# Attention, a dense layer and a routed layer of eight experts: half of the first expert's products set between the last routing's, and range checks, one weight piece and routing placed elsewhere

## The chip, the cores and the metric

One core of one Trainium2 chip. The metric is device time in microseconds (us) of one execution, the median of several; lower is better. Engines are TensorE (PE, with its weight loads as PEld), VectorE (DVE), ScalarE (ACT), GpSimd (POOL) and SyncE (SP, which issues most DMAs).

## What is computed

Three layers, each on the output of the one before; 4 sequences of 768 positions, 3072 tokens of 384 values.

```python
# 1: a gated linear recurrence for each of 8 heads of 48
for t in range(S):
    S_re, S_im = ar * S_re - ai * S_im + kv, ar * S_im + ai * S_re
    y[:, :, t] = einsum('bhd,bhde->bhe', q[:, :, t], S_re)
# 2: a product of two projections to 1536, and one back
x = ((x @ w_a) * (x @ w_b)) @ w_out
# 3: tokens with x @ w_skip > 0 go to the one expert with the largest logit
e_idx = argmax(xc @ w_gate, axis=1)
y[mask] = gate_w[mask, None] * (maximum(xc[mask] @ w1[e], 0) @ w2[e])   # 384 -> 1024 -> 384
out[do_compute] = xc + y
```

## The kernel before

The recurrence is worked in 24 units of 128 positions (6 chunks of 4 sequences), two units to a group, 12 groups. A group's 256 tokens then go through the dense layer (`moe1`): twelve steps f, each with 18 products of 256 columns for `ab{g}_f` and six of 394 columns (`op`, L631 to L633) for the step before last. All products work on operands split into a high and a low part in `fp32r`, three products for one. Between them, DVE and ACT make `asb`, `gh`, `gl` of the step, and the trigonometry, exponentials and masks of the next group's units.

The last ten of the 394 columns are the gate and skip logits. Routing of a group has three parts: `pick` (the expert's one-hot `rt_oh`, and on PE the prefix sums `pp`), `weigh`, and `place` (`sl`, the comparison of a row's position with 256 slots, and on PE the products `pt` that add the group's tokens to the slot table `tbl`; for the last group `pt` for the indices `giu` and `pg` for the gate values). The `xr` rows of a group are written to a table `xd` in DRAM (L676) and to `out`.

Each expert takes 256 slots: `gather` fetches two times 128 rows of `xd` by indirect DMAs on POOL, `tokens` transposes them on PE (`xgp`) and splits them (`xgt`), `hidden` makes eight blocks of nine products of 256 columns (`eh`, L954 to L957), with a Relu on ACT (`hh`) and the low part on DVE (`hl`), and `second` six products of 384 columns for each block (`eo`, L971 to L973, into two banks, one for each 128 rows). The first expert's weights (`wq0` to `wq3`) are in place in group 11; the next ones are loaded into `stg` (six loads of 768 KB, gated by a small POOL copy from the first gathered rows) and converted by `convert`, ACT making the high part and DVE or POOL the low one.

The order on each engine is a scheduler's, held by rows of names: `ORDER` for the start, `STEADY` for the groups from 3 on, with a word such as `asb{g}_1` for one instruction; `chain` ties each named instruction behind the one before. `PLACE` (a row for each operation, `wl` being the low part of the ten logit columns `wo` takes from `w2s`, L532) names the engine of an instruction where it isn't the usual one.

Two things need checks that the reference doesn't have: `least` and `largest` (L285, L288) test the range of `a_re` and `a_im`. Units 0 to 5 are tested late, by `check_late` in groups 2 to 4: a second load into `chk` (one buffer, L294, behind `ts` of a later unit), then the test on DVE. If a test fails, or an expert has more than 256 tokens, a slow branch is taken behind the main block.

`warm` issues bf16 products of 128x256 that nobody reads: 10 behind group 11's last product, 6 behind its prefix sums, 24 behind the gate products, 13 and 8 behind the first expert's two transposes, 61 in all (`WARMS`, `WARMX`, L837).

Of the kernel before, what the change touches and what calls it, by code (L numbers as in the profile page):

```python
# [10 lines left out]
F32 = mybir.dt.float32  # L11
F32R = mybir.dt.float32r
# [48 lines left out]
    "wl": {"vector": (1, 4,)},  # L61
# [15 lines left out]
WARMS = (10, 6, 24)  # L77
WARMX = (13, 8)
ENGINES = {getattr(mybir.EngineType, x) for x in ("PE", "Activation", "DVE", "Pool")}
GF = 5  # L80
PORT = 8
ROWS = 64
# [14 lines left out]
    "DVE": "q{u} k{u} q{v} k{v} t4_{u} asb{g}_0 lg{p}*2 tl{u} t4_{v} gl{g}_0 tl{v} asb{g}_1 t3_{u}*2 gl{g}_1 t4_{u} asb{g}_2 qr{u}:1 kr{u}:1 gl{g}_2 t3_{v}*2 qr{u}:0 kr{u}:0 asb{g}_3 t4_{v} gl{g}_3 kr{v}:1 asb{g}_4 kr{v}:0 gl{g}_4 qr{v}:1 qr{v}:0 asb{g}_5 gl{g}_5 sc{u}_0 sc{u}_1 xt{n} asb{g}_6 gl{g}_6 t1_{x} t1_{y} asb{g}_7 t1_{x} ll{x} gl{g}_7 t1_{y} ll{y} asb{g}_8 gl{g}_8 sc{v}_0 sc{v}_1 im{x} imp{x} im{y} imp{y} xt{n} asb{g}_9 gl{g}_9 re{a} re{b} asb{g}_10 gl{g}_10 asb{g}_11 gl{g}_11",  # L97
}


def keep_rows(nc, after):
# [34 lines left out]
def kern(tc, q, k, v, a_re, a_im, w_a, w_b, w_out, w_skip, w_gate, w1, w2, out):  # L136
# [3 lines left out]
    with st:  # L140
# [148 lines left out]

        def check_late(i):  # L290
            c, b = units[i]
            for src, test in ((a_re, least), (a_im, largest)):
# [3 lines left out]
                test(i, t)  # L296
# [329 lines left out]
        def moe1_out(g, f, gh, gl):  # L626
# [7 lines left out]
            if f == NF - 1:  # L634
                moe1_end(g)
                if g == NG - 1:
                    warm("m", i.ins, WARMS[0])

        def moe1_step(g, f):
# [15 lines left out]
            dve.tensor_tensor(out=asb, in0=ab[:, 256:], in1=asb, op=ALU.mult)  # L655
# [10 lines left out]
        def moe1_end(g):  # L666
# [40 lines left out]
        def pick(g, behind=None, spare=None):  # L707
            if g == NG - 1:
                whole()
# [28 lines left out]
            if g == NG - 1:  # L738
                warm("p", i.ins, WARMS[1])
# [55 lines left out]
        def slots(tiles, tag, sls, last=False, spare=None):  # L795
# [29 lines left out]
            warm("t", ins.ins, WARMS[2])  # L825

# [163 lines left out]
        def experts(first):  # L990
# [21 lines left out]
            for e in range(2):  # L1012
                gather(e)
# [282 lines left out]
```

## Time and profile before

| | us |
|---|---|
| median of 3 runs | 832.45 (832.26 to 834.45) |
| the profiled execution | 831.85 |
| its span | 830.0 |
| PE busy | 786.5 |
| PEld busy | 754.2 |
| DVE busy | 550.4 |
| ACT busy | 453.0 |
| POOL busy | 167.6 |

The mean granted clock of PE is 0.997 of full speed. The times of single instructions come from the profiled execution, so sums are made against its 831.85 us. Matmuls are pipelined: the time of one in a row is longer than the distance between the starts of two. PE's idle time is the first thing to look for, then what released PE at its end.

### The profile page before, as it was taken

Reading aid. Unit: us, or ns where it says so; the run is one execution under the profiler, and the core shown is the slowest. Engines: PE = TensorE matmul, PEld = TensorE weight load, DVE = VectorE, ACT = ScalarE, POOL = GpSimd, SP = SyncE. Lnnn points to the kernel's source line nnn. Section 1 sums busy time; section 2 is a strip of 40 time slices with the busy share of each in tenths; the row PEclk is TensorE's granted clock in tenths of the full one; section 3 lists DMA queues with packets and bytes.
Section 4 is the critical chain, followed back from the end, with each engine's and each line's share of the span. In section 5 each row is a group of like instructions: output and inputs, shape, how many; then the busy total and the mean of one; then the engine's idle time right before and its main releaser. Section 6 shows DMA issues by size and latency. Waiting matters only on the chain.

```text
span 830.0 us, 22382 instructions
## 1 busy us (share of the span) xinstructions
PE 786.5 (95%) x9115; PEld 754.2 (91%) x9115; DVE 550.4 (66%) x1417; ACT 453.0 (55%) x949; POOL 167.6 (20%) x196
## 2 busy tenths in 40 slices
PE   1899999999999999999999999999999999999995
PEld 0589899999989989999999999998999989999995
DVE  7999888685676857757676576746747347555541
ACT  6897655473546644566455565555535226555540
POOL 3131443410100000000000000000003026666650
PEclk9999999999999999999999999999999999999998
DMA  9995223251342432213222231120105049667500
GB/s 253 251 316 121 54 63 68 46 122 33 77 89 38 106 64 72 54 36 87 51 68 55 52 81 36 50 49 11 40 18 176 1 164 338 215 222 208 180 22 23
DMA packets 180960, 83.17 MB, mean 100 GB/s; under 512 B 152084, under 2 KB 168026, under 8 KB 180848
## 3 DMA queue, kind: packets, MB, share of 16 engines
q1 hardware_dynamic: 178800, 76.26, 35.7%
q0 software_dynamic: 2048, 5.40, 1.8%
q8 instruction: 73, 1.20, 0.6%
q14 instruction: 39, 0.32, 0.1%
HBM read 69.84 MB, written 12.61 MB: 99 GB/s over the span
## 4 chain that ended last, share of the span: by engine, by line
PE 80%; DVE 6%; DMA 6%; ACT 3%; issue 2%; POOL 1%; SPq 0%; POOLq 0%; DVEq 0%; ACTq 0%
PE ab L647 11%; PE ab L648 10%; PE ab L649 10%; PE op L632 5%; PE op L631 5%; PE op L633 5%; PE y L502 4%; PE eh L954 3%; PE eh L955 3%; PE eh L957 3%; PE eo L971 3%; PE eo L972 3%; PE eo L973 3%; DMA chk<-in_a_im_dram 2%; PE pcs L461 2%
## 5 line engine op out<-in xcount | busy, mean ns | idle before, releaser
L647 PE MATMUL ab<-xt,wa 128*128 128x256 f32 x432 | 124.4, 288 | 0.5 <-DVE asb L655 0.4
L647 PE MATMUL ab<-xt,wb 128*128 128x256 f32 x432 | 123.0, 285 | 0.1
L648 PE MATMUL ab<-xt,wb 128*128 128x256 f32 x432 | 122.5, 284 | 0.0
L649 PE MATMUL ab<-xt,wb 128*128 128x256 f32 x432 | 122.4, 283 | 0.0
L649 PE MATMUL ab<-xt,wa 128*128 128x256 f32 x432 | 121.7, 282 | 0.0
L648 PE MATMUL ab<-xt,wa 128*128 128x256 f32 x432 | 121.6, 281 | 0.0
L659 DVE TENSOR_TENSOR gl<-asb,gh 128x256 fp32r<-128x256 f32 x131 | 62.6, 478 | 64.0 <-ACT gh L279 63.9
L632 PE MATMUL op<-wo,gh 128*128 128x394 f32 x288 | 99.2, 344 | 1.7 <-POOL wo L532 1.7
L633 PE MATMUL op<-wo,gh 128*128 128x394 f32 x288 | 98.7, 343 | 0.0
L631 PE MATMUL op<-wo,gl 128*128 128x394 f32 x288 | 98.5, 346 | 0.0
L279 ACT ACTIVATE asb<-ab 128x256 f32<-128x256 f32 x139 | 52.5, 378 | 68.8 <-PE ab L649 65.2
L647 PEld LDWEIGHTS ab<-xt,wa 128*128 128x128 f32 x432 | 81.4, 188 | 2.4 <-ACT asb L279 0.7
L648 PEld LDWEIGHTS ab<-xt,wb 128*128 128x128 f32 x432 | 81.5, 189 | 1.1 <-issue 1.0
L655 DVE TENSOR_TENSOR asb<-ab,asb 128x256 f32<-128x256 f32 x144 | 60.0, 417 | 33.3 <-ACT asb L279 33.1
L647 PEld LDWEIGHTS ab<-xt,wb 128*128 128x128 f32 x432 | 81.4, 188 | 0.6 <-DVE wb L532 0.3
L649 PEld LDWEIGHTS ab<-xt,wb 128*128 128x128 f32 x432 | 81.3, 188 | 0.7 <-issue 0.6
L648 PEld LDWEIGHTS ab<-xt,wa 128*128 128x128 f32 x432 | 81.4, 188 | 0.5 <-DVE xt L514 0.2
L649 PEld LDWEIGHTS ab<-xt,wa 128*128 128x128 f32 x432 | 81.5, 189 | 0.3 <-issue 0.2
L922 POOL TENSOR_TENSOR wq<-stg,wq 128x768 fp32r<-128x768 f32 x32 | 59.5, 1861 | 95.7 <-DMA stg<-in_moe_w_dram 46.4
L279 ACT ACTIVATE gh<-asb 128x256 fp32r<-128x256 f32 x132 | 54.4, 413 | 36.3 <-DVE asb L655 36.1
L264 POOL MEMSET v<- 128x64 f32 x24 | 3.5, 150 | 339.0 <-PE y L502 246.3
L961 DVE SCALAR_TENSOR_TENSOR hl<-eh,hh 128x256 fp32r<-128x256 f32 x64 | 27.1, 424 | 52.9 <-ACT hh L960 52.8
(268 smaller groups left out, 2021.2 us busy)
## 6 DMA issues: line engine op xcount, KB each, us to landing
stg<-in_moe_w_dram SPq DMA_DIRECT2D x28, 768.0 KB
rawa<-in_moe_w_a_dram SPq DMA_DIRECT2D x6, 768.0 KB
re<-in_a_re_dram SPq DMA_DIRECT2D x24, 192.0 KB
rawb<-in_moe_w_b_dram SPq DMA_DIRECT2D x6, 768.0 KB
q<-in_q_dram SPq DMA_DIRECT2D x24, 192.0 KB
k<-in_k_dram SPq DMA_DIRECT2D x24, 192.0 KB
rawo<-in_moe_w_out_dram SPq DMA_DIRECT2D x6, 768.0 KB
xd<-xr SPq DMA_DIRECT2D x24, 192.0 KB
```

The costliest lines, as they stand in the source:

```text
L279: return act.activation(out=out, in_=in_, func=AF.Copy) if e is act else e.tensor_copy(out, in_)
L502: ins = pe.matmul(o, l[:, col : col + STRIP], r, start=begin, stop=end).ins
L631: pe.matmul(o, gl[:, ts], wh, start=f == 0, stop=False)
L632: pe.matmul(o, gh[:, ts], wl, start=False, stop=False)
L633: i = pe.matmul(o, gh[:, ts], wh, start=False, stop=f == NF - 1)
L647: pe.matmul(o, wl, xt[:, c, 0], start=c == 0, stop=False)
L648: pe.matmul(o, wh, xt[:, c, 1], start=False, stop=False)
L649: pe.matmul(o, wh, xt[:, c, 0], start=False, stop=c == NCC - 1)
L655: dve.tensor_tensor(out=asb, in0=ab[:, 256:], in1=asb, op=ALU.mult)
L659: on("gl", n).tensor_tensor(out=gl, in0=asb, in1=gh, op=ALU.subtract)
L922: lo.tensor_tensor(out=o[:, 1], in0=t, in1=o[:, 0], op=ALU.subtract)
L961: vm = dve.scalar_tensor_tensor(out=gl, in0=o, scalar=0.0, in1=gh, op0=ALU.max, op1=ALU.subtract)
```

## The change

- `wl` names piece 3 for DVE; DVE's row of `ORDER` has `wo3` between the two `kr3`, and POOL's row loses it.
- `STEADY` holds from group 2 on. In its DVE row the second `t1_{y}` stands ahead of `ll_{x}`, and the table's addition `tbl:{r}` is named ahead of `asb{g}_9`. The trigonometry of units 6 and 7 is issued in two steps, as that of later pairs.
- The late tests are tied one by one behind `asb` of steps 1, 4, 7 and 10 of groups 2 to 4.
- New rows `LAST` (PE) and `LAST_DVE` set the end of group 11. Routing of group 10 fills a first half of expert 0's slots; its 128 rows are gathered in group 11 (`gather_half`, by `gi0`, a copy of the indices), and transposed behind `ab11_10`. A third flag, `good[:, 2]`, says that these 128 slots are all taken; if not, the slow branch is run. The rows of group 10 are also written over group 11's places of `xd`, two writes of 192 KB more, before group 11's own.
- Expert 0's products for f = 0 to 5 are made for each 128 rows apart: `front(h, x)`, 36 products of 128 columns for x = 0 and 18 for x = 1 (`fa{h}_x`), with a Relu and a low part of 128x512 and 128x256; `back(h, f)`, three of 384 columns. `front(0, 0)`, `front(0, 1)` and three `back(0, f)` stand between the last routing's products; the others, `hidden(0, 6)`, `hidden(0, 7)` and their `second` follow when the second half is gathered. From expert 1 on the loop is as before. Only one gather, of the second half, stands ahead of expert 1's two, and the loads of `stg` are gated on it.
- The 61 warming products are gone.

```diff
-    "wl": {"vector": (1, 4,)},
+    "wl": {"vector": (1, 3, 4,)},
...
-WARMS = (10, 6, 24)
-WARMX = (13, 8)
+TESTS = (1, 4, 7, 10)
...
+LAST = "ab11_3*18 pp10*3 ab11_4*18 pt9*4 ab11_5*18 pt10*4 ab11_6 ab11_10*18 xgp0_0*3 ab11_11*18 op11_1:35 fa0_0*12 pp11*3 fa0_0*10 pt11*8 fa0_0*14 fa0_1*18 eo0_0*3 pg11*4 eo0_0*6"
+LAST_DVE = "lg11*2 m11 sk11 eq11*2 m211 rt_oh:22*2 dl11 rt_r:44*2 psl11*2 sl22 sl23 giu gt11*3 rt_r:46*2 fh0*2"
...
-        for g in range(3, NG - 1):
+        for g in range(2, NG - 1):
...
-                test(i, t)
+                tests.append(test(i, t).ins)
...
-            if 2 * p >= PORT:
+            if 2 * p >= CAUSAL:
...
-            dve.tensor_tensor(out=asb, in0=ab[:, 256:], in1=asb, op=ALU.mult)
+            i = dve.tensor_tensor(out=asb, in0=ab[:, 256:], in1=asb, op=ALU.mult).ins
+            if g >= 2 and f in TESTS and tests:
+                after(tests.pop(0), i)
...
                 xw = sync.dma_start(xd[r0 : r0 + P, :], xr[:, t]).ins
+                if g == NG - 2:
+                    r0 = tok0(2 * g + 2 + t)
+                    sync.dma_start(xd[r0 : r0 + P, :], xr[:, t])
...
+        def front(h, x):
+            hs = slice(h * P, (h + 1) * P)
...
+            for n in range((4, 2)[x]):
+                on_ = o[:, n * P : (n + 1) * P]
+                for c in range(NCC):
+                    wh, wl = (wv[:, y, c, n * P : (n + 1) * P] for y in range(2))
+                    pe.matmul(on_, wl, xgt[0][:, c, 0, hs], start=c == 0, stop=False)
+                    pe.matmul(on_, wh, xgt[0][:, c, 0, hs], start=False, stop=False)
+                    pe.matmul(on_, wh, xgt[0][:, c, 1, hs], start=False, stop=c == NCC - 1)
...
+            act.activation(out=gh, in_=o, func=AF.Relu)
+            dve.scalar_tensor_tensor(out=gl, in0=o, scalar=0.0, in1=gh, op0=ALU.max, op1=ALU.subtract)
...
+        def back(h, f):
...
+            pe.matmul(o, gl, wh, start=f == 0, stop=False)
+            pe.matmul(o, gh, wl, start=False, stop=False)
+            pe.matmul(o, gh, wh, start=False, stop=False)
...
+                tokens(0, 1)
+                for f in range(3, 6):
+                    back(0, f)
+                front(1, 0)
+                for i in range(2):
+                    convert()
+                front(1, 1)
+                convert()
+                last_ = [hidden(0, 6)]
+                convert()
+                for f in range(4):
+                    back(1, f)
+                last_.append(hidden(0, 7))
+                gather(2)
+                tokens(1, 0)
+                convert()
+                for f in range(4, 6):
+                    back(1, f)
+                tokens(1, 1)
...
+                if g == NG - 1:
+                    for x in range(2):
+                        front(0, x)
                 for r in sorted(lgs):
                     route(r)
+                if g == NG - 1:
+                    for f in range(3):
+                        back(0, f)
+                if g == NG - 2:
+                    whole()
...
+                    dve.tensor_copy(good[:, 2:], t6[:, 0, 2, :1])
+                    dve.tensor_copy(gi0, t6[:, 0, 1, :1])
+                    gather_half(0, gi0, env.left)
+                    tokens(0, 0)
```

What stands on the engines, at three places. First PE behind the last product of group 11, where `pp11` are the prefix sums of the last routing. Before:

```order
L837 LDWEIGHTS ones_119
L837 MATMUL warmm_10394<-iota_115,ones_119 128x256
L735 LDWEIGHTS ustrict_121
L735 MATMUL pp11_10419<-rt_oh_132,ustrict_121 128x16
L736 LDWEIGHTS ones_119
L736 MATMUL pp11_10419<-rt_oh_132,ones_119 128x8
L737 LDWEIGHTS ones_119
L737 MATMUL pp11_10419<-ohs_124,ones_119 128x16
L837 LDWEIGHTS ones_119
L837 MATMUL warmp_10423<-iota_115,ones_119 128x256
```

The six rows of `pp11` stand behind the tenth warming product, and further warming products follow. With the change:

```order
L976 MATMUL fa0_0_10412<-xgt0_10009,wq0_9495 128x128
L977 MATMUL fa0_0_10412<-xgt0_10009,wq0_9495 128x128
L745 LDWEIGHTS ustrict_121
L745 MATMUL pp11_10486<-rt_oh_132,ustrict_121 128x16
L746 LDWEIGHTS ones_119
L746 MATMUL pp11_10486<-rt_oh_132,ones_119 128x8
L747 LDWEIGHTS ones_119
L747 MATMUL pp11_10486<-ohs_124,ones_119 128x16
L975 MATMUL fa0_0_10412<-xgt0_10009,wq0_9495 128x128
L976 MATMUL fa0_0_10412<-xgt0_10009,wq0_9495 128x128
```

`pp11` stands behind twelve products of `fa0_0`, and ten more follow before the index products. Second, DVE in group 2, from a test of unit 0 on (`chk`, `immax`) to the masked scores `sc6_0` of unit 6, which PE needs. Before:

```order
L288 TENSOR_REDUCE immax_87<-chk0_2662 128x1
L318 SCALAR_TENSOR_TENSOR t1_8_3068<-t1_8_3068,t2_8_3069 128x384
L312 TENSOR_TENSOR t1_9_3097<-t1_9_3097,t2_9_3098 128x384
L655 TENSOR_TENSOR asb2_4_2814<-ab2_4_2789,asb2_4_2814 128x256
L327 TENSOR_TENSOR ll8_3082<-t1_8_3068,lh8_3081 128x384
L285 TENSOR_SCALAR chk1_2665,remin_88<-chk1_2665 128x384
L329 TENSOR_TENSOR im8_2253<-im8_2253,t2_8_3069 128x384
L659 TENSOR_TENSOR gl2_4_2819<-asb2_4_2814,gh2_4_2817 128x256
L655 TENSOR_TENSOR asb2_5_2846<-ab2_5_2821,asb2_5_2846 128x256
L470 TENSOR_TENSOR sc6_0_2394<-pcs0_2188,keep_86 128x512
```

Between the test of unit 0's `a_im` and `sc6_0` stands the first test of unit 1, `chk1`. With the change:

```order
L290 TENSOR_SCALAR chk0_2661,remin_88<-chk0_2661 128x384
L384 TENSOR_SCALAR t4_7_2298<-t3_7_2297 128x384
L666 TENSOR_TENSOR gl2_3_2789<-asb2_3_2784,gh2_3_2787 128x256
L398 TENSOR_TENSOR kr7_2335<-k7_2170,ts7_2330 128x8x48
L660 TENSOR_TENSOR asb2_4_2816<-ab2_4_2791,asb2_4_2816 128x256
L396 TENSOR_TENSOR kr7_2335<-k7_2170,t4_7_2298 128x8x48
L293 TENSOR_REDUCE immax_87<-chk0_2664 128x1
L666 TENSOR_TENSOR gl2_4_2821<-asb2_4_2816,gh2_4_2819 128x256
L396 TENSOR_TENSOR qr7_2332<-q7_2168,t4_7_2298 128x8x48
L660 TENSOR_TENSOR asb2_5_2848<-ab2_5_2823,asb2_5_2848 128x256
L666 TENSOR_TENSOR gl2_5_2853<-asb2_5_2848,gh2_5_2851 128x256
L477 TENSOR_TENSOR sc6_0_2396<-pcs0_2190,keep_86 128x512
```

Both tests of unit 0 stand there, the first behind `asb2_3`, and those of unit 1 have moved behind `sc6_0`. Third, DVE where the low part of `wo3` now stands. Before:

```order
L582 COPY w2s3_1042<-wt3_1_1053 128x10
L659 TENSOR_TENSOR gl0_7_1165<-asb0_7_1160,gh0_7_1163 128x256
L389 TENSOR_TENSOR kr3_781<-k3_184,t4_3_766 128x8x48
L391 TENSOR_TENSOR kr3_781<-k3_184,ts3_776 128x8x48
L526 TENSOR_SCALAR deca5_1333<-deca5_1333 128x768
```

And with the change:

```order
L589 COPY w2s3_1044<-wt3_1_1055 128x10
L666 TENSOR_TENSOR gl0_7_1167<-asb0_7_1162,gh0_7_1165 128x256
L396 TENSOR_TENSOR kr3_783<-k3_186,t4_3_768 128x8x48
L539 TENSOR_TENSOR wo3_1041<-w2s3_1044,wo3_1041 128x2x10
L398 TENSOR_TENSOR kr3_783<-k3_186,ts3_778 128x8x48
L533 TENSOR_SCALAR deca5_1335<-deca5_1335 128x768
```

One small instruction has come in between the two `kr3`.

## Rows read from the trace of the kernel before

**Rows 1.** The page, part 1: busy us, share of the span, instructions.
```profile
PE 786.5 (95%) x9115; PEld 754.2 (91%) x9115; DVE 550.4 (66%) x1417; ACT 453.0 (55%) x949; POOL 167.6 (20%) x196
```

**Rows 2.** Windows of groups 2-5, 11: length, engines' busy us (count), PEclk, DMA share.
```profile
163.47:216.35 52.88, 51.30 (x719) 49.35 (x719) 34.76 (x106) 27.00 (x63) 5.48 (x8) 1.00 0.34 73
216.35:267.97 51.62, 50.47 (x719) 48.28 (x719) 36.41 (x116) 30.42 (x67) 2.71 (x5) 1.00 0.36 75
267.97:321.25 53.28, 51.26 (x721) 49.25 (x720) 36.43 (x107) 28.58 (x65) 2.10 (x4) 1.00 0.34 72
321.25:371.93 50.68, 50.68 (x721) 49.07 (x720) 34.88 (x101) 28.83 (x66) 2.08 (x4) 1.00 0.28 61
625.63:668.29 42.66, 41.45 (x308) 40.93 (x307) 22.30 (x64) 15.49 (x36) 6.39 (x4) 1.00 0.24 75
```

**Rows 3.** PE's timeline: start, us, line, op, [idle before <-releaser].
```profile
91.41 0.45 PE L632 MATMUL op<-wo,gh 128*128 128x394 f32 x1 [1.67 <-POOL wo L532]
...
187.02 0.30 PE L502 MATMUL y<-sc,v 128*32 128x128 f32 x1 [1.58 <-DVE sc L470]
...
243.67 0.17 PE L735 MATMUL pcs<-rt_oh,ustrict 128*128 128x16 bf16 x1 [0.81 <-DVE rt_oh L728]
...
297.06 0.17 PE L735 MATMUL pcs<-rt_oh,ustrict 128*128 128x16 bf16 x1 [2.02 <-DVE rt_oh L728]
...
641.29 0.20 PE L803 MATMUL pt<-rt_r,sl 128*128 128x48 bf16 x1 [1.21 <-DVE sl L789]
```

**Rows 4.** Timeline of all engines, end of group 11 to expert 0.
```profile
668.11 0.34 PE L633 MATMUL op<-wo,gh 128*128 128x394 f32 x1
...
669.50 0.36 DVE L728 SCALAR_TENSOR_TENSOR rt_oh<-eq,m,sk 128x8 bf16<-128x8 f32 x2
...
670.57 0.48 DVE L789 TENSOR_SCALAR sl<-iota,rt_pos 128x256 bf16<-128x256 bf16 x2
...
671.44 0.17 DVE L822 TENSOR_TENSOR giu<-tbl,pt 128x16 uint32<-128x16 f32 x1
...
672.50 0.22 PE L816 MATMUL pg<-rt_r,sl 128*128 128x24 bf16 x3
...
676.08 0.52 PE L938 MATMUL xgp<-ident,xg 128*128 128x128 f32 x3 [0.72 <-DMA xg<-xd,giu]
...
677.85 0.49 PE L938 MATMUL xgp<-ident,xg 128*128 128x128 f32 x3
...
678.97 0.37 PE L954 MATMUL eh<-xgt,wq 128*128 128x256 f32 x1
```

**Rows 5.** Windows, PE alone, from expert 0's first product on.
```profile
678.95:696.50 17.55, 17.55 (x130) 1.00 1.01 358
```

**Rows 6.** Timelines of DVE and POOL: the low part of two wo pieces.
```profile
63.91 0.17 DVE L532 TENSOR_TENSOR wo<-w2s,wo 128x20 fp32r<-128x20 f32 x1
...
88.12 3.24 POOL L532 TENSOR_TENSOR wo<-w2s,wo 128x20 fp32r<-128x20 f32 x1 [4.22 <-ACT wo L279]
```

**Rows 7.** The chain of waits, in order of time: start, us, what.
```profile
239.03 3.14 DMA chk<-in_a_im_dram
...
283.61 4.96 DMA chk<-in_a_im_dram
```

**Rows 8.** DVE's waits, 80 to 310 us: total, times, longest.
```profile
DVE immax L288 <- DMA chk<-in_a_im_dram: 7.2, 4, 2.3
```

**Rows 9.** PE's timeline, six products of 384 columns, nine of 256, the next.
```profile
693.69 0.34 PE L971 MATMUL eo<-wq,hl 128*128 128x384 f32 x1
...
694.75 0.28 PE L954 MATMUL eh<-xgt,wq 128*128 128x256 f32 x1
...
695.80 0.34 PE L971 MATMUL eo<-wq,hl 128*128 128x384 f32 x1
```

**Rows 10.** DVE's timeline in group 11.
```profile
635.66 1.85 DVE L659 TENSOR_TENSOR gl<-asb,gh 128x256 fp32r<-128x256 f32 x1 [0.67 <-ACT gh L279]
```

**Rows 11.** PE's timeline: plain f32 products near the start.
```profile
21.60 2.93 PE L358 MATMUL tp<-t,trit 128*128 128x384 f32 x4 [3.98 <-ACT t L230]
```

More of the change, by code (lines that the diff above doesn't have):

```diff
@@ L117, in keep_rows @@
         row = []
-        for g in range(3, NG - 1):
-            row += words.format(p=g - 1, g=g, n=g + 1, u=2 * g + 2, v=2 * g + 3, x=2 * g + 4, y=2 * g + 5, a=2 * g + 6, b=2 * g + 7).split()
+        for g in range(2, NG - 1):
+            row += words.format(p=g - 1, r=g - 2 if g > 2 else 9 * NG, g=g, n=g + 1, u=2 * g + 2, v=2 * g + 3, x=2 * g + 4, y=2 * g + 5, a=2 * g + 6, b=2 * g + 7).split()
         chain(writers, after, engine, row)
+    chain(writers, after, "PE", LAST.split())
+    chain(writers, after, "DVE", LAST_DVE.split())
 def chain(writers, after, engine, words):
@@ L288, in largest @@
             return dve.tensor_reduce(out=immax[:, i : i + 1], in_=im, axis=AX.X, op=ALU.max, apply_absolute_value=True)
+        tests = []
         def check_late(i):
@@ L707, in pick @@
         def pick(g, behind=None, spare=None):
-            if g == NG - 1:
+            if g == NG - 1 and not halves:
                 whole()
@@ L830, in whole @@
             dve.tensor_tensor(out=t6[:, :, 1], in0=t6[:, :, 1], in1=t6[:, :, 0], op=ALU.add)
-        def warm(name, ins, n):
-            if n:
-                wm = bank("op", f"warm{name}", 2)
-                for x in range(n):
-                    after(pe.matmul(wm[:, :CAP], ones, iota, start=True, stop=True).ins, ins)
         giu = cpool.tile([P, 2, NE], U32, name="giu")
@@ L876, in indices, with gather_half, row_half @@
             dve.tensor_tensor(out=gate, in0=gate, in1=tg[:, :, 2], op=ALU.add)
+        good = cpool.tile([P, 3], F32, name="good")
+        gi0 = cpool.tile([P, 1], U32, name="gi0")
         xgs = {}
+        halves = {}
+        def gather_half(h, rows, home):
+            halves[h] = home.tile([P, DM], F32, tag=f"xgh{h}", name=f"xgh{h}", bufs=1)
+            pool.indirect_dma_start(
+                out=halves[h], out_offset=None, in_=xd[:, :],
+                in_offset=bass.IndirectOffsetOnAxis(ap=rows, axis=0),
+                bounds_check=NTOK - 1, oob_is_err=False,
+            )
+        def row_half(e, h):
+            return halves[h] if e == 0 and halves else xgs[e][:, h]
         def gather(e):
@@ L1010, in convert @@
                         stage()
-            for e in range(2):
-                gather(e)
+            if first:
+                gather_half(1, giu[:, 1, :1], env.right)
+            else:
+                gather(0)
+            gather(1)
             for i in range(NSTG):
-                stage(xgs[0][:, 0, :1] if first else None)
+                stage(halves[1][:, :1] if first else None)
             for i in range(0 if first else 8):
                 convert()
-            for h in range(2):
-                ins = tokens(0, h)
-                if first:
-                    warm(f"x{h}", ins, WARMX[h])
             pend = []
-            for e in range(NE):
+            if first:
+                tokens(0, 1)
[17 more added lines that the diff above has]
+                tokens(1, 1)
+                convert()
+                second(*last_[0])
+                convert()
+                second(*last_[1])
+                convert()
+            else:
+                for h in range(2):
+                    tokens(0, h)
+            for e in range(first, NE):
                 for f in range(NEF):
                     pend.append(hidden(e, f))
-                    for i in range((0, 0, 1, 1, 1, 1, 2, 2)[f] if e == 0 else 1):
+                    for i in range(1):
                         convert()
@@ L1154, in kern @@
         pb = at("pbad")
-        pe.matmul(pb[:, :2], ones, goodb, start=True, stop=True)
-        dve.tensor_reduce(out=todo_f[:, 1:2], in_=pb[:, :2], axis=AX.X, op=ALU.add)
-        dve.tensor_scalar(out=todo_f[:, 1:2], in0=todo_f[:, 1:2], scalar1=float(2 * P), scalar2=None, op0=ALU.is_lt)
+        pe.matmul(pb[:, :3], ones, goodb, start=True, stop=True)
+        dve.tensor_reduce(out=todo_f[:, 1:2], in_=pb[:, :3], axis=AX.X, op=ALU.add)
+        dve.tensor_scalar(out=todo_f[:, 1:2], in0=todo_f[:, 1:2], scalar1=float(3 * P), scalar2=None, op0=ALU.is_lt)
         count_rounds(1)
```

31 lines of the change are left out of this document (21 added, 10 removed), and 2 rows, old and new, of the table ORDER.

## The prediction

> **What bounds the kernel now.** I read the page first. TensorE (PE) is busy for 786.5 of 830.0 us [rows 1], so a change is worth what it takes out of PE's idle time, or out of work that PE does without need. The windows by group come second. Group 5 takes 50.68 us, and PE is busy in all of it; groups 2, 3 and 4 take 52.88, 51.62 and 53.28 us and hold 1.58, 1.15 and 2.02 us in which PE does nothing [rows 2]. PE's timeline names what ended each of these gaps [rows 3]. Third, the stretch from the last product of group 11 (668.11) to the first of expert 0 (678.97), where PE runs 61 warming matmuls whose result nobody reads, in batches, and waits between them, for the gathered rows last [rows 4]. From 678.95 on PE is full: 17.55 of 17.55 us [rows 5].
>
> **1. The 10-column low part of wo3, moved from POOL to DVE.** The POOL instruction took 3.24 us, from 88.12, and PE stood 1.67 us until it ended; another of the same on DVE took 0.17 us [rows 3, 6]. PE would have gone on at 91.41 - 1.67 = 89.74. DVE's row puts the small operation between the two kr3, so it is issued in a stretch in which DVE has other work, and costs 0.17 us there. Bounds: 0 (it comes up late, or the next small wait takes the gain back) and -1.67. I take **-1.0**.
>
> **2. The late range checks, and the order of groups 2 to 4.** Today the four tests of a group's two units follow each other. They share one buffer, so each load starts only when the test before it is over. In group 3 a load of 3.14 us lies between two tests, and rt_oh, for which PE waits 0.81 us at 243.67, stands behind them; group 4 has the same with loads of up to 4.96 us and 2.02 us of waiting; in group 2 it is sc that comes late, by 1.58 us [rows 3, 7]. DVE stood 7.2 us for these loads in all [rows 8]. The change ties the four tests of a group behind asb of f = 1, 4, 7 and 10. From one to the next is 3 steps; a step is 18 products some 0.117 apart and 6 some 0.177 apart (nine of expert 0's in 1.05 us, six of its second kind in 1.06 [rows 9]), 3.2 us, so 9.5 us, while a load with its test needs 3 to 5.5 us: each load has landed long before its test comes up. In group 2 two tests instead of three stand ahead of sc. The same twelve tests are made, and nothing is added to PE. Were a test still to wait, the next asb would be queued behind it, and PE behind that. Bounds: the excess of the three groups over group 5, 2.20 + 0.94 + 2.60 = -5.7, and half of PE's gaps in them (1.58 + 1.15 + 2.02 = 4.75), -2.4, if the new order of group 2, which now follows the steady row, meets a wait of its own. I take **-4.5**. That the trigonometry of units 6 and 7 is issued in two steps is an order on ACT in the same groups, and inside these bounds.
>
> **3. Routing inside group 11.** PE stands 1.21 us at 641.29 for sl, in step 4 [rows 3]. DVE was late there: a gl took 1.85 us in place of some 0.4 [rows 10]. The change sets these four products behind the 18 of step 5, at least a step of 3.2 us later, and DVE's delay fits into that. Bounds 0 and -1.21; I take **-1.2**.
>
> **4. The first 128 rows of expert 0.** Before: the last product of group 11 starts at 668.11 and the next could start at 668.29. PE reaches expert 0 at 678.97 [rows 4]. Expert 0 has 72 products 0.118 apart and 48 that are 0.176 apart (by the window of 17.55 us, which also holds six transposes of expert 1, 0.66, and by the spacings [rows 5, 9]) = 8.50 + 8.45 = 16.95; with the transposes it is done, at the equivalent, at 678.97 + 17.6 = **696.6**. After: the list of PE from 668.29 on, in its new order, is
> - 54 half-width products for each half, f = 0 to 5: 108 x p;
> - the hidden blocks 6 and 7 in full width, 18 x 0.118 = 2.12;
> - the second products of f = 0 to 5, 18 for each half, 36 x 0.176 = 6.34, and those of 6 and 7, 12 x 0.176 = 2.11;
> - transposes of the second half, 0.33, and of expert 1, 0.66;
> - the last routing's small ones, some 20: three of pg take 0.22, the last one's own duration in it [rows 4], so under 20 x 0.073 = 1.5; I take 0.7.
>
> No 128-column product with split operands is in the trace of before. The line through the spacings at 256 and 384 columns (0.118 and 0.176) gives 0.060 at 128; the other end is 0.118, since a product of 256 columns, with weights of the same size to load, is spaced at that [rows 9]. The nearest row is the transposes of 128x128: three in 0.49, less one duration of 0.27, are 0.11 apart [rows 4]. I take **p = 0.111**, so 11.99. The sum is 24.25, and 0.33 more for the first half's transposes, which move up into group 11: 668.29 + 24.6 = 692.9 against 696.6, **-3.7**.
>
> Nothing of this list should wait long. Its first 12 products end at 669.6; rt_oh was done at 669.86, so the prefix products wait 0.2 us. The index products come ten products later, at 671.1, and sl was done at 671.05; so giu is where it was, at 671.44, and the second half is there by 676.1, as today [rows 4]. Until then PE has the rest of fa0_0, fa0_1 and nine second products, 32 x 0.111 + 9 x 0.176 + 0.15 behind 671.4, that is to 676.7. The first half's rows depend on groups 0 to 10 alone; by the reference's inputs 153 of expert 0's 169 tokens are in these, more than the 128 needed, so the branch for too few is not taken. The two further writes of 192 KB and the early gather fall into group 11, where DMA is 0.24 busy [rows 2]; POOL has one gather there and then one fewer before expert 1's loads, which may start a good 1 us sooner. At p = 0.118 the part is worth -2.9; at 0.060 it is -7.0, as PE then waits from 675.1 to 676.1 for the second half.
>
> The warming matmuls cost nothing in this account, as they stood in gaps. With them the clock was 1.00 [rows 2, 5]; after it PE has real products there, with gaps under 0.3 us.
>
> By the Trainium skill, "TensorE: Matmul & The Clock Gate", section "LDWEIGHTS (loading the stationary operand)", halving the moving columns saves little: a load goes by the 128 columns of the weights, 107 ns, whatever streams after it. By that figure part 4 would be -4.1. The page's section "Back-to-back issue gap" has 81 ns for a stream of 128-column products; by that it would be -5.8. The trace's 0.11 agrees with the first; both lie between the bounds that the rows give.
>
> **The sum.** -1.0 - 4.5 - 1.2 - 3.7 = -10.4 us. The profiled execution was at 831.85 (span 830.0): 821.45. The median of the runs, 832.45, stands 0.6 above it, so **822.0**.
>
> **Rivals.**
> (a) *The waits come back elsewhere* (0.17). DVE, busy for 36.4 of the 51.6 us of group 3 [rows 2], is late at another product instead: part 2 gives -2.4, parts 1 and 3 together -0.5, part 4 -2.9, in all -5.8 and **826.6**; with a new wait of 2 us in part 4, **828.6**. For it: DVE stands behind most of the gaps. Against it: group 5, with the same steady order and no tests, has no gap at all.
> (b) *The half-width products fall to the rate of plain f32*, the case on the other side (0.08). Four plain f32 products of 128x384 took 2.93 us [rows 11], 0.73 each against 0.176 for the split ones; by columns that is 0.244 for 128. Part 4 is then -3.7 + 108 x (0.244 - 0.111) = +11.0, the whole -6.7 + 11.0 = +4.3: **836.7**. It is slower from p = 0.21 on, where part 4 eats the other three. Against it: at 256 and at 384 columns both run at 0.46 ns a column, with no sign of a step.
> (c) *The last routing slips* (0.05). Its prefix, index and gate products now stand in PE's queue behind 12, 22 and 57 of expert 0's; what makes these late, a Relu or a subtraction of the first half that comes up late on ACT or DVE, moves giu and the second half's gather with it, and PE stands behind the nine second products. With 3.7 us of that, part 4 is 0 and the whole -6.7: **825.7**. Against it: up to the index products nothing but fa0_0 stands ahead, whose operands are ready since group 11's last step.
>
> **How the numbers follow.** The forecast has 0.70, (a) 0.17, (b) 0.08, (c) 0.05. Its own bounds are -1.7 - 5.7 - 1.2 - 7.0 = -15.6 and 0 - 2.4 - 0 - 2.9 = -5.3, that is 816.8 to 827.1. With (c) and most of (a) the range is **816.5 to 828.8**; (b) and the rest of (a) are left out. 0.3% (2.5 us) is what a measurement of this kernel can tell from no change, so faster means under 829.95. There lie the forecast, (c) and nearly all of (a): 0.88. 0.05 is for no difference, from the ends of (a) and the low end of (b), and 0.07 for slower, the rest of (b).
>
> **What would show it.** PE's gaps at 91, 187, 243 and 297 us gone, groups 2 to 4 at 50.7 to 51.2 us each, and no wait of immax for chk over 0.5 us. The gap at 641 gone. The products named fa0 and fa1 0.10 to 0.12 apart; giu still 3.2 to 3.5 us behind the last product of group 11; expert 1's first hidden products some 24.3 us behind it. I am wrong if fa is spaced by over 0.15, if PE shows more than 1 us of idle time between 668 and 695, if its clock falls there, or if groups 2 to 4 stay above 51.5.

## The result, and the profile after

The changed kernel takes **822.75 us** (median of 4 runs, 822.36 to 823.39) against 833.16 for the kernel before beside it; the ratio is 0.9875, with a 95% interval of 0.9857 to 0.9892. The forecast was 822.0. The profiled execution ran 823.1 us, its span is 821.4. The time was met, but not by the terms of the sum: two of the four fell short by 2 us or more, and against them stand 1.0 us of a gain sized too low and 2.5 us of gains left out. That these nearly cancel is luck.

The page of the changed kernel, parts 1 and 2 (first the engines' busy time, then the granted clock in 40 slices), to set against [rows 1]:

```profile
PE 782.5 (95%) x9108; PEld 753.8 (92%) x9108; DVE 549.4 (67%) x1418; ACT 451.4 (55%) x947; POOL 164.7 (20%) x195
...
PEclk9999999999999999999999999999999999999998
```

PE's busy time fell by only 4.0 us, its idle time from 43.5 to 38.9: 61 unread products went, but halving expert 0's products brought some back. The slices are too coarse to show the slow stretch that the windows below do.

Where the 8.6 us between the two spans went shows best by groups. This table is made from the start of the first `ab` product of each group in the two traces (between groups 0 and 1, whose steps interleave, of the 217th):

| stretch | before | after | difference | forecast |
|---|---|---|---|---|
| up to group 0 | 46.27 | 46.06 | -0.21 | |
| group 0 | 58.57 | 56.59 | -1.98 | -1.0 (wo3) |
| group 1 | 58.62 | 58.48 | -0.14 | |
| groups 2 / 3 / 4 | 52.89 / 51.61 / 53.28 | 50.82 / 54.27 / 51.08 | -2.07 / +2.66 / -2.20 | -4.5 together |
| groups 5 to 9 | 255.19 | 253.35 | -1.84 | 0 |
| group 10 | 49.18 | 48.86 | -0.32 | 0 |
| group 11, to its last `ab` product | 39.31 | 38.61 | -0.70 | -1.2, and +0.33 from part 4 |
| from there to the end | 165.10 | 163.28 | -1.82 | -4.0 (part 4, less that 0.33) |

The same in windows of the changed kernel: stretch, length, busy time of PE, PEld, DVE, ACT and POOL with their counts, granted clock, DMA. They answer to [rows 2]:

```profile
161.13:211.95 50.82, 49.85 (x714) 47.80 (x713) 33.48 (x101) 27.46 (x62) 5.31 (x8) 1.00 0.36 76
211.95:266.22 54.27, 51.50 (x725) 49.12 (x724) 37.85 (x120) 29.38 (x69) 2.84 (x5) 1.00 0.36 76
266.22:317.30 51.08, 50.73 (x720) 49.09 (x720) 36.37 (x108) 28.34 (x63) 1.20 (x3) 1.00 0.33 70
```

Group 3 alone has grown: PE stands 2.77 of its 54.27 us. PE's timeline names every gap that is left behind group 0 and over 0.5 us (these answer to [rows 3]):

```profile
169.48 0.44 PE L276 MATMUL tp<-tl,tri_r 128*128 128x384 f32 x1 [0.72 <-DVE tl L369]
...
260.95 0.38 PE L652 MATMUL ab<-xt,wa 128*128 128x256 f32 x1 [0.68 <-DVE asb L660]
...
264.94 0.45 PE L638 MATMUL op<-wo,gl 128*128 128x394 f32 x1 [1.66 <-DVE gl L666]
...
566.79 0.44 PE L276 MATMUL l<-ll,tri_r 128*128 128x384 f32 x1 [0.56 <-DVE xt L521]
...
690.16 0.36 PE L1003 MATMUL eh<-xgt,wq 128*128 128x256 f32 x1 [1.86 <-DVE hl L1010]
```

The gaps at 91, 187, 243, 297 and 641 us are gone, as forecast. Three are new: 0.72 at 169, in group 2 (for `tl`, from DVE), and 0.68 and 1.66 in group 3. The one at 690, in expert 1's first blocks, behind all that the change had moved, has grown: in before PE waits 1.06 us for hl at the same block, and DVE takes 4.68 us for a conversion ahead of it, next to two on POOL. Before:

```profile
700.19 0.36 PE L954 MATMUL eh<-xgt,wq 128*128 128x256 f32 x1 [1.06 <-DVE hl L961]
```

```profile
695.04 4.68 DVE L922 TENSOR_TENSOR wq<-stg,wq 128x768 fp32r<-128x768 f32 x1 [0.31 <-ACT wq L921]
```

```profile
695.23 3.65 POOL L922 TENSOR_TENSOR wq<-stg,wq 128x768 fp32r<-128x768 f32 x2
```

The stretch that part 4 is about, in PE's timeline, to set against [rows 4]: the last product of group 11, two half-width products nine apart, the second half's transposes, and expert 1's first product:

```profile
661.30 0.34 PE L640 MATMUL op<-wo,gh 128*128 128x394 f32 x1
...
670.09 0.53 PE L953 MATMUL xgp<-ident,xgh 128*128 128x128 f32 x3
...
676.01 0.28 PE L975 MATMUL fa<-xgt,wq 128*128 128x128 f32 x1
...
677.02 0.27 PE L975 MATMUL fa<-xgt,wq 128*128 128x128 f32 x1
...
686.08 0.28 PE L1003 MATMUL eh<-xgt,wq 128*128 128x256 f32 x1
```

Nine half-width products take 1.01 us: 0.112 each. From the last product of group 11 to expert 1 it is 24.78 us, of which PE stands 0.18; in before, to the equivalent point, 696.6 - 668.11 = 28.5.

The late tests still wait for their loads now and then, the longest time here:

```profile
286.30 0.55 DVE L293 TENSOR_REDUCE immax<-chk 128x1 f32<-128x384 f32 x1 [1.60 <-DMA chk<-in_a_im_dram]
```

PE has no gap over 0.5 us in that group.

### The profile page after: what moved, and what is told of

It reads as the page before. It is cut to its first block, busy times and chain, and to the rows that moved or that the text cites. A ratio compares the mean times of both kernels' runs of the same rounds, so it can differ in the third digit from the quotient of the medians.

```text
span 821.4 us, 22341 instructions
## 1 busy us (share of the span) xinstructions
PE 782.5 (95%) x9108; PEld 753.8 (92%) x9108; DVE 549.4 (67%) x1418; ACT 451.4 (55%) x947; POOL 164.7 (20%) x195
## 4 chain that ended last, share of the span: by engine, by line
PE 92%; DVE 3%; ACT 2%; issue 1%; DMA 1%; SPq 1%; POOLq 0%; POOL 0%; DVEq 0%; ACTq 0%
PE ab L652 13%; PE ab L653 12%; PE ab L654 12%; PE op L638 6%; PE op L639 6%; PE op L640 6%; PE y L509 5%; PE pcs L468 3%; PE eo L1020 3%; PE eo L1022 3%; PE eo L1021 3%; PE eh L1003 2%; PE eh L1004 2%; PE eh L1006 2%; PE ds L419 1%; PE pq L450 1%
## 5 line engine op out<-in xcount | busy, mean ns | idle before, releaser
L1010 DVE SCALAR_TENSOR_TENSOR hl<-eh,hh 128x256 fp32r<-128x256 f32 x58 | 24.5, 423 | 49.3 <-ACT hh L1009 49.3
```

## Experiments

Each run was timed with runs of the kernel before on the same chip, so ratios compare best between kernels; the changed kernel's is 0.9875. Most ratios are known to some 0.25% (2 us) either way, so where two kernels differ by less, the argument rests on windows of their traces, one execution each.

**Group 3: the table's addition.** DVE's timeline of the changed kernel at the end of group 3 (idle time and releaser in brackets) shows what asb waited behind; the line of 1.28 us is ACT's:

```profile
257.82 0.25 DVE L812 TENSOR_TENSOR tbl<-tbl,pcs 128x96 f32<-128x96 f32 x1
257.98 0.28 DVE L797 TENSOR_SCALAR sl<-iota,rt_pos 128x256 bf16<-128x256 bf16 x1
260.31 0.25 DVE L812 TENSOR_TENSOR tbl<-tbl,pcs 128x96 f32<-128x96 f32 x1 [2.04 <-PE pcs L811]
260.48 0.41 DVE L660 TENSOR_TENSOR asb<-ab,asb 128x256 f32<-128x256 f32 x1
...
261.49 1.28 ACT L208 ACT_TABLE_LOAD   x1
...
264.06 0.82 DVE L666 TENSOR_TENSOR gl<-asb,gh 128x256 fp32r<-128x256 f32 x1 [3.17 <-ACT gh L284]
```

Two routings, of groups 0 and 1, are added to the table here, through one PSUM bank (`pcs`), so the second's products follow the first's addition. The new word in the steady row holds the second addition ahead of asb of step 9. PE's gap of 0.68 us follows from that directly; the one of 1.66 comes a step later, as ACT took four exponentials, the load of a table and two more operations before it made gh from the late asb, and gl waited 3.17 us for it.

```diff
-            row += words.format(p=g - 1, r=g - 2 if g > 2 else 9 * NG, g=g, n=g + 1, u=2 * g + 2, v=2 * g + 3, x=2 * g + 4, y=2 * g + 5, a=2 * g + 6, b=2 * g + 7).split()
+            row += words.format(p=g - 1, r=g - 2 if g > 3 else 9 * NG, g=g, n=g + 1, u=2 * g + 2, v=2 * g + 3, x=2 * g + 4, y=2 * g + 5, a=2 * g + 6, b=2 * g + 7).split()
```

> The changed kernel with one edit: the steady DVE row names the table's addition from group 4 on instead of 3. Theory: group 3 became 2.7 us longer because two routings share one PSUM bank there, both additions are held ahead of asb3_9, and DVE waits 2.04 us for the second's products. Then without the tie group 3 falls from 54.3 to 51.0-51.5 us, PE's two gaps near 261 and 265 us (0.68 and 1.66) go, and the kernel takes 820.0-820.8 (2.2-2.8 us under 822.75). Rival: the tests tied behind asb3_7 and asb3_10 make DVE late; then group 3 stays at 53.5 or more and the time at 822-823.

Measured: 821.1 us, ratio 0.9841 (0.9817 to 0.9866); the median is just above the range expected. Both gaps are gone. The windows of groups 3 and 4 of this kernel:

```profile
211.91:264.67 52.76, 52.06 (x731) 50.37 (x730) 39.06 (x123) 26.62 (x64) 1.19 (x3) 1.00 0.35 73
264.67:315.09 50.42, 50.05 (x715) 47.71 (x714) 35.89 (x104) 30.78 (x68) 3.28 (x5) 1.00 0.36 76
```

Together 103.2 us against 105.35. Group 3 did not come down to the 51.0 to 51.5 us expected: more products fall into its window (731 against 725), and 0.70 us is left in which PE waits for nothing that the profile shows (0.43 in the changed kernel). The additions are where the loss was; the tied tests, still in place, were not.

**The tests tied, the old rows kept.** The changed kernel with `STEADY` from group 3 on and its DVE row in the old words (no `tbl`, `ll` of the first unit ahead of the second `t1`), and the trigonometry of units 6 and 7 in one step.

> The changed kernel with the tests tied as in the change, but the steady rows from group 3 on, in their old words, and the trigonometry of units 6 and 7 in one step. If the ties alone hold the gain of groups 2 to 4, the gaps at 187, 243 and 297 us stay away, group 3 takes 51.0-51.5 us (no gap at 261 and 265), and the time is 820-821. If the new rows are needed for group 2 (the rival), group 2 stays at 52 us or more and the time is 822-824.

Measured: 822.68 us, ratio 0.9865 (0.984 to 0.989). Its windows of groups 2 to 4, and the one large gap of PE in them:

```profile
160.44:212.75 52.31, 51.35 (x719) 48.99 (x719) 34.49 (x106) 26.98 (x63) 5.56 (x8) 1.00 0.35 74
212.75:263.87 51.12, 50.39 (x719) 48.22 (x718) 36.54 (x116) 30.35 (x67) 2.68 (x5) 1.00 0.36 76
263.87:314.73 50.86, 50.86 (x721) 49.12 (x720) 36.20 (x107) 28.99 (x65) 2.06 (x4) 1.00 0.36 76
```

```profile
183.39 0.30 PE L509 MATMUL y<-sc,v 128*32 128x128 f32 x1 [0.96 <-DVE sc L477]
```

So there are two pieces, and the rival's numbers came (group 2 over 52, 822 or more). The ties do the work in groups 3 and 4: 101.98 us, 2.9 under before, and no wait left for rt_oh. In group 2 they take only 0.6 of 2.1 us; the rest needs the new rows there or the two-step trigonometry, which this run took out together. On groups 5 to 9 the old rows take 254.83 us, 1.5 more than the new ones: that gain, which the forecast put at 0, is the new row's, by the order of `t1` and `ll` or by the word for the table, which no run took apart. All in all the rows gave as much as they took, and the time is the changed kernel's.

**wo3 alone.** The kernel before with `"wl": {"vector": (1, 3, 4,)}` and `wo3` in DVE's row.

> The kernel before with wo3's small low part on DVE and nothing else. If the 2.0 us that group 0 lost in the changed kernel come from this alone, group 0 takes 56.6 us (58.6 before), the gap at 91 us is gone, everything behind keeps its length, and the time falls by 1.9-2.2 us, to some 831. Rival: the next wait takes part of it back without the rest of the change: 57.0 us or more and under 1.5 us of gain.

Measured: 832.37 us beside 834.14, ratio 0.998 (0.9969 to 0.9991). Group 0 takes 56.66 us, 1.9 under before, and PE has no gap at 91 us. So the gain in group 0 is this edit's alone. What was not expected: in the profiled execution (833.61, the second slowest of ten) group 2 was 1.9 us longer than in before's and group 4 0.4, with the gaps of [rows 3] at 1.96 and 2.79 in place of 1.58 and 2.02:

```profile
185.95 0.30 PE L502 MATMUL y<-sc,v 128*32 128x128 f32 x1 [1.96 <-DVE sc L470]
...
297.92 0.17 PE L735 MATMUL pcs<-rt_oh,ustrict 128*128 128x16 bf16 x1 [2.79 <-DVE rt_oh L728]
```

The longer gap is 0.4 of group 2's 1.9 us. Behind it PE runs slow, which before's execution does not show behind its 1.58 (windows of all engines; the granted clock is the third number from the end):

```profile
188.00:190.00 2.00, 2.00 (x16) 1.76 (x19) 2.00 (x10) 0.65 (x3) 0.00 (x0) 0.50 0.51 98
```

With 0.85 and 0.79 in the windows beside it, that is 0.3 + 1.0 + 0.42 = 1.7 us of PE's time. Behind the gap of 2.79 the clock stayed at 1.00. So the waits, and what the clock does behind them, are not the same from execution to execution, and the part of the gain that arrives at the end differs (the ten runs lie between 831.93 and 833.94).

**Without parts 3 and 4.** The kernel before with wo3, the ties, the new steady rows and the two-step trigonometry; no `front`, `back`, `LAST` or early gather, and the warming products in place.

> The kernel before with wo3, the tied tests, the new steady rows and the two-step trigonometry, but expert 0 whole behind the last routing, the warming products kept and group 11 in its old order. Groups 2 to 4 together 156.2 us and groups 5 to 9 some 1.8 us under before, as in the changed kernel. The rest of the change is then the difference to it. By my sum of the two traces it is 0.7 (group 11) + 1.8 (behind it): 825-826. If the halves are worth the 3.7 us forecast and the wait at 690 is chance, 827 or more; if they are worth nothing, 823 or less.

Measured: 827.71 us beside 834.14, ratio 0.9924 (0.9906 to 0.9942); the changed kernel is at 0.9875, so parts 3 and 4 are worth about 0.5%, 4 us. By the number that is the upper outcome, but not by its reason: the wait at 690 isn't chance. The three profiled executions that keep that order (the changed kernel's, the one with the addition named later and the one with the old rows) show 1.86 to 1.87 us, and this run, without it, 1.08 at the same block. Groups 2 to 4 take 156.7 us together, as expected, but groups 5 to 9 are only 1.1 us under before, not 1.8. The traces also say less than 4, as the two profiled executions differ by 1.8 us ahead of group 10, where their order is the same: from group 10's first product on it is 253.8 us here and 250.7 with the halves.

**The gap at 690.** DVE and POOL of the changed kernel ahead of it, in one timeline:

```profile
685.94 1.86 POOL L937 TENSOR_TENSOR wq<-stg,wq 128x768 fp32r<-128x768 f32 x1
686.18 2.45 DVE L937 TENSOR_TENSOR wq<-stg,wq 128x768 fp32r<-128x768 f32 x1 [0.67 <-ACT wq L936]
688.55 1.13 DVE L1028 SCALAR_TENSOR_TENSOR xgh<-eo,gate,xgh 128x384 f32<-128x384 f32 x2
...
689.60 0.41 DVE L1010 SCALAR_TENSOR_TENSOR hl<-eh,hh 128x256 fp32r<-128x256 f32 x1
```

A conversion that takes 0.96 us by itself (at 677.58, for one) took 2.45 next to one on POOL, expert 0's two closing operations followed, and only then came hl of expert 1's first block, which frees the bank for its third. Behind the gap PE is slow (windows as above):

```profile
688.00:690.00 2.00, 0.29 (x3) 0.09 (x1) 2.00 (x5) 1.44 (x3) 0.56 (x1) 1.00 0.75 156
690.00:692.00 2.00, 1.84 (x11) 1.87 (x12) 1.21 (x3) 0.28 (x1) 1.68 (x3) 0.75 1.05 406
692.00:694.00 2.00, 2.00 (x9) 2.00 (x8) 1.55 (x2) 0.84 (x2) 2.00 (x2) 0.50 0.21 75
694.00:696.00 2.00, 2.00 (x16) 2.00 (x15) 2.00 (x1) 0.88 (x2) 1.39 (x1) 0.89 0.49 103
```

At 0.75, 0.50 and 0.89 of full speed (0.50 is 1.2 in place of 2.4 GHz), these six microseconds lose 0.50 + 1.00 + 0.22 = 1.7 us of PE's time. Whether the kernel loses them too is a question for the run on the clock below. The first edit moves both things that stand ahead of hl; as each call takes the next conversion in line, two calls less set all later ones two blocks back:

```diff
                 second(*last_[0])
-                convert()
-                second(*last_[1])
-                convert()
+                pend.append(last_[1])
```

> The changed kernel, but expert 0's last six second products follow expert 1's first hidden blocks, and two weight conversions come two blocks later. Theory: PE's 1.86 us gap at 690 comes from hl of expert 1's first block standing on DVE behind a conversion of 2.45 us and expert 0's two closing operations; the granted clock then falls to 0.50 for some 3 us, which costs about 1.6 us more. Both go: 819.3-820.3, and the clock stays at 1.00 from 680 to 700. Rival: DVE and POOL slow each other wherever the conversions stand; then a gap of over 1 us appears at one of the next blocks and the time stays within 1 us of 822.75.

Measured: 820.16 us, ratio 0.9838 (0.9812 to 0.9863), PE without a gap over 0.2 us behind 665 and a clock of 1.00 from 680 to 700. From group 11's last `ab` product to the end it is 160.2 us against 163.28. The rival, a new wait further on, did not come. Which of the two it is, two further runs tell.

```diff
                 second(*last_[0])
-                convert()
                 second(*last_[1])
-                convert()
```

> The changed kernel with only the two conversions two blocks later; expert 0's second products stay ahead of expert 1's first block. If the conversion of 2.45 us ahead of hl is what makes PE wait at 690, the gap falls under 0.5 us, the clock stays at 1.00 and the kernel takes 819.8-820.5, as with both edits. If expert 0's two closing operations on DVE (1.13 us) count as much, a gap of 0.5-1.1 us stays and the time is 821 or more.

Measured: 819.81 us, ratio 0.9826 (0.9802 to 0.985), no gap over 0.2 us behind 665, and 159.97 us from group 11's last `ab` product to the end. The conversions alone are enough.

```diff
                 second(*last_[0])
                 convert()
-                second(*last_[1])
                 convert()
+                pend.append(last_[1])
```

> The changed kernel with only expert 0's last six second products behind expert 1's first hidden blocks; the conversions stay. The closing operations then stand behind hl, the conversion of 2.45 us ahead of it. If the conversion is the cause, PE still waits 1 us or more for hl in expert 1's first three blocks, and the time is 821-823; if the closing operations are, 820.5 or less.

Measured: 827.06 us, ratio 0.9913 (0.9886 to 0.9939): 4 us slower than the changed kernel, worse than any outcome I had written down. Its PE, DVE and POOL:

```profile
693.77 0.55 PE L1003 MATMUL eh<-xgt,wq 128*128 128x256 f32 x1 [4.31 <-DVE hl L1010]
```

```profile
687.33 5.96 DVE L937 TENSOR_TENSOR wq<-stg,wq 128x768 fp32r<-128x768 f32 x1 [0.67 <-ACT wq L936]
693.21 0.41 DVE L1010 SCALAR_TENSOR_TENSOR hl<-eh,hh 128x256 fp32r<-128x256 f32 x1
```

```profile
687.08 5.39 POOL L937 TENSOR_TENSOR wq<-stg,wq 128x768 fp32r<-128x768 f32 x3
```

In the changed kernel POOL stores expert 0's closed rows (L1029, from 689.43) between its conversions; with the closing operations later the stores are too, DVE's conversion met three of POOL's in a row, and lasted until 0.8 us behind the last of them. The changed kernel's did the same behind one: POOL's ended at 687.80, DVE's at 688.63. The Trainium skill has a rule for this in "SBUF — State Buffer", section "Summary: rules for kernel authors": where a DVE operation has two inputs in SBUF and a GpSimd one reads SBUF, the second to issue "fully blocks" until the first is done. These rows agree, as DVE's started 0.24 and 0.25 us behind POOL's. In before, at 695, DVE's conversion starts 0.19 us ahead of POOL's by the profile and waits through both all the same, so the starts that a profile shows don't always tell which of the two waits.

**The clock alone.** Sixteen unread products of 128x256 behind expert 1's second block, where PE stood.

```diff
+                    if first and (e, f) == (1, 1):
+                        wm = bank("at", "warmz", 2)
+                        for x in range(16):
+                            after(pe.matmul(wm[:, :CAP], ones, iota, start=True, stop=True).ins, pend[-1][4][0])
```

> The changed kernel with 16 unread bf16 products of 128x256 (about 1.7 us) behind expert 1's second hidden block, where PE stood 1.86 us. Theory: the gap itself is not shortened, but the clock stays at 1.00 behind it, so the kernel gains the price of the slow clock alone: 1.2-1.7 us, 821.0-821.6. Rival: the clock falls there whatever PE does (load of the whole core), then nothing is gained: 822.5-823.2 with 0.50 still in the windows from 691 to 694.

Measured: 823.61 us, ratio 0.9877 (0.9852 to 0.9902): no gain. Yet the clock stayed at 1.00 in every window from 686 to 708, so what I expected of the clock held and what I expected of the time did not. Most of the 1.7 us came back as a wait eight microseconds later, behind a conversion that met three of POOL's:

```profile
698.65 0.39 PE L1003 MATMUL eh<-xgt,wq 128*128 128x256 f32 x1 [1.11 <-DVE hl L1010]
```

```profile
692.80 5.46 DVE L937 TENSOR_TENSOR wq<-stg,wq 128x768 fp32r<-128x768 f32 x1 [0.31 <-ACT wq L936]
```

The run with the table's addition named later shows the same without filler. Its PE waits 1.87 us at the same block, the clock stays at 1.00 behind that in this execution, and the second wait comes:

```profile
688.50 0.36 PE L1003 MATMUL eh<-xgt,wq 128*128 128x256 f32 x1 [1.87 <-DVE hl L1010]
...
696.80 0.39 PE L1003 MATMUL eh<-xgt,wq 128*128 128x256 f32 x1 [1.11 <-DVE hl L1010]
```

```profile
690.00:692.00 2.00, 2.00 (x18) 2.00 (x16) 1.47 (x2) 1.00 (x3) 1.98 (x3) 1.00 0.36 136
```

From group 11's last `ab` product to the end it is 162.84 us there and 162.88 with the filler, against 163.28 and, with the old rows, 163.31 in the two executions with the slow clock. So DVE, not PE, set the pace of expert 1's first blocks, and of the slow clock's 1.7 us the kernel lost some 0.4.

**The warming products alone.** The kernel before with `WARMS = (0, 0, 0)` and `WARMX = (0, 0)`.

> The kernel before without its 61 warming products. Theory from the gap at 690 us of the changed kernel (the clock fell to 0.50 behind 1.86 us without products, for about 3 us): the clock falls in the stretch from 668 to 679 and expert 0 starts slow; 3-4 us at half clock cost 1.5-2 us: 834.5-836. Rival: PE waits for the gather in that stretch anyway and the clock recovers within it, the time stays at 832.5-833.5.

Measured: 836.27 us beside 834.14, ratio 1.0023 (1.0012 to 1.0034): 1 to 2.8 us slower. PE's longest wait there is 3.48 us, for the gathered rows at 679.18; the windows of all engines around it:

```profile
674.00:676.00 2.00, 0.71 (x14) 0.48 (x12) 1.81 (x19) 0.00 (x0) 0.29 (x1) 0.79 0.45 162
676.00:678.00 2.00, 0.00 (x0) 0.00 (x0) 0.88 (x6) 0.00 (x0) 1.70 (x2) 0.50 0.19 30
...
682.00:684.00 2.00, 1.73 (x8) 1.76 (x9) 0.56 (x1) 0.17 (x1) 0.00 (x0) 0.50 0.89 231
684.00:686.00 2.00, 2.00 (x14) 2.00 (x14) 0.42 (x1) 0.38 (x1) 0.00 (x0) 0.65 1.04 399
```

The clock fell to 0.50 and stayed there until expert 0 had run for some 3 us. From group 11's last `ab` product to the end the trace has 167.1 us against 165.1. So the warming products earned about 2 us in before. In the changed kernel products that are needed stand in their place, and its clock is 1.00 in every window from 660 to 690 without them.

**Both mends.** The changed kernel with `r` from group 4 on and the first edit of the gap at 690.

> The changed kernel with both edits: the table's addition named from group 4 on, and expert 0's last second products behind expert 1's first hidden blocks with two conversions later. If the two gains add up (1.7 and 2.6-3 us by their medians and traces), 817.5-818.5, with groups 3 and 4 at 103.2 us and no gap of PE near 690. Rival: DVE is the bound of expert 1's first blocks, and what group 3 gives is waited for there: 819.5 or more.

Measured: **817.78 us** (817.12 to 817.93), ratio 0.9802 (0.9788 to 0.9817), the fastest of all. Its windows of groups 3 and 4, and from 680 to 700:

```profile
212.06:264.27 52.21, 52.04 (x730) 50.35 (x730) 39.08 (x123) 26.61 (x64) 1.19 (x3) 1.00 0.35 74
264.27:314.78 50.51, 49.90 (x714) 47.70 (x714) 35.92 (x104) 30.80 (x68) 3.30 (x5) 1.00 0.36 76
680.00:700.00 20.00, 20.00 (x148) 19.97 (x147) 11.77 (x20) 12.37 (x23) 14.98 (x12) 1.00 0.77 257
```

The two gains add up: 0.9875 - 0.9802 is 0.7%, 6 us, and the spans say the same (821.4 and 815.4); alone, the two edits shorten their stretches by 2.2 and 3.1 us in the traces.

## Why the prediction was right, and where its steps were not

**Part 1 (wo3), -1.0 forecast, -2.0 measured.** The mechanism held, and two sizes were off. The 1.0 left room for some waiting for DVE's version, but PE did not wait at all; and the bound of -1.67, the length of the gap, was too tight, as group 0 became 0.3 us shorter than the gap alone gives. Where these 0.3 us come from is open.

**Part 2 (groups 2 to 4), -4.5 forecast, -1.6 measured**, outside the bounds of -5.7 to -2.4. The step on the ties was right for PE: the gaps that stood behind tests are gone, and with the old rows the ties gave -3.5 us. That each load has landed "long before its test comes up" was not: the first two tests of a group came 3.8 to 5.2 us apart, where the working had 9.5, and one still waited 1.60 us for its load. What failed in the time is the step that "the new order of group 2" could only cost a wait "of its own" in that group: the same rows now name `tbl` in group 3, where two routings share a bank, and that cost 2.7 us. I had weighed the words of the row for group 2, and not what group 3 would make of them. Undoing that one word gave 2 us back in groups 3 and 4.

**Left out: groups 5 to 9, -1.8 us.** The sum left these groups out, with their gaps of 0.42 and 0.91 us at 566 and 573. The new steady row removed the first and shortened the second to 0.56; the other 1.1 us stand in no gap of PE. The run with the old words lost 1.5 of the 1.8 us. Which of the words it was is open.

**Part 3, -1.2 forecast.** -0.70 in group 11 with 0.33 of added transposes: -1.0, and the gap at 641 is gone. Near the forecast, by one pair of executions; no run has this part alone, and the other executions with this order take 38.5 to 39.1 us for the stretch where this one took 38.61.

**Part 4, -3.7 forecast, -1.5 measured** (-1.82 behind group 11's last `ab` product, +0.33 in group 11). Its sum held to the end of expert 0: 24.78 us behind the start of group 11's last product where the list said 24.4, with p = 0.112 where I took 0.111, no rival price, and giu 3.5 us behind the last product. "Nothing of this list should wait long" held too, with 0.18 us of idle time. What failed lies behind the list, where the sum put nothing: all from expert 1 on was to keep its length, 830.0 - 696.6 = 133.4 us, and it took 821.4 - 686.08 = 135.3. These 1.9 us went at expert 1's first blocks. The wait for hl grew from 1.06 to 1.86 us, and what DVE and POOL convert behind it holds hl up once more, which shows as a wait of 1.11 us where the clock stays up and is hidden in the slow products where it falls. Setting the conversions two blocks back took both away. The trace of before had the collision in view, in the 4.68 us conversion and the wait of 1.06 us behind it. Of the rivals, (a) had this in its end, "a new wait of 2 us in part 4". The Trainium skill's page "TensorE: Matmul & The Clock Gate" puts a load of 128 columns of weights at 128 / 1.2 = 107 ns ("LDWEIGHTS (loading the stationary operand)") and a stream of 128-column products at about 81 ns each ("Back-to-back issue gap"): the measured 0.112 us agrees with the first and not with the second.

**The warming products.** "Cost nothing in this account" was right in the changed kernel, where the clock stayed at 1.00 through the stretch; taken out alone they are worth 2 us.

**The sum.** By the spans the gain was 8.6 us, not 10.4: errors of -1.0, +2.9, +0.2 and +2.2 in the four parts, and -2.5 left out. That the medians do give 10.4 has to do with which executions were profiled: before's was 1.3 us under its median beside the change, the changed kernel's 0.35 us over its own. In rival (b), -3.7 + 108 x (0.244 - 0.111) is +10.7, not +11.0, which changes nothing here.

**Its own signs.** Of the prediction's four signs of being wrong only the spacing of fa stayed away (0.112 us). PE stood 1.86 us at 690, its clock fell there, and group 3 stayed above 51.5 us; a test waited 1.60 us, where it had allowed 0.5. The mechanisms of parts 1 and 3 held, and that of part 4 up to the end of expert 0; that the time was met as closely as 0.75 us was luck.

## What to carry to other kernels

When a row of order is extended to stages that it didn't cover, read what each word names in every one of them: here a single word cost more than the whole of part 1 gave. When work is pulled forward, follow the sum one stage past its end: what comes sooner meets the next stage's helpers in another phase, and the price stood on DVE and POOL, which converted weights at the same time. And filler for an idle PE pays only where PE is what the next stage waits for; the same 16 products that kept the clock up gained nothing where DVE was late.

## What the runs showed of the hardware

The granted clock fell to half (0.50, 1.2 in place of 2.4 GHz) behind some gaps of PE and not behind others as long. It fell behind 1.61 us (the run with the conversions alone, at 265), 1.86 (the changed kernel, at 690, for some 3.5 us), 1.87 (old rows) and 1.96 (wo3 alone, at 186). It stayed at 1.00 behind 1.66 (the changed kernel, the same gap at 265), 1.87 (the addition named later, at 688), 2.02 (before, at 297) and 2.79 (wo3 alone, at 298), and behind every wait of 1.06 to 1.11 us in expert 1. Ahead of the gaps at 690 and 688 PE had been busy for over 20 us without a gap over 0.2 us, and the clock did one thing in one execution and the other in the other. So in these rows the length of a gap from 1.6 to 2.8 us does not tell by itself what the clock does. Without the warming products several waits in a row, the longest of 3.48 us, brought some 10 us below full speed. What a slow stretch costs depends on what bounds there: some 1.5 us of group 2's length (wo3 alone), some 0.4 in expert 1's first blocks.

A DVE conversion with both inputs in SBUF doesn't share with one on POOL but waits for it: 0.96 us alone, 2.45 next to one POOL conversion, 4.68 next to two (before), 5.46 and 5.96 next to three in a row.

A product of 128 columns with split operands was spaced at 0.112 us against 0.117 for 256 columns, so halving the columns saved next to nothing: expert 0's blocks 0 to 5 cost 108 x 0.112 = 12.1 us in place of 54 x 0.117 = 6.3. Starting them early paid for these 5.8 us, as in before PE had 10.7 us there (668.29 to 678.97) with only the last routing's small products, the transposes and unread ones.
